# The last stores of an attention and channel-mix kernel: one queue for all turned results, and the very last result transposed by TensorE in two halves

## The chip, the cores and the metric

The kernel runs on one core of a Trainium2 chip. The metric is the device time of one execution in microseconds (us), the median of several runs; lower is better. Engines are named as in the profile: PE is TensorE (PEld its weight loads), DVE is VectorE, ACT is ScalarE, POOL is GpSimd, SP is SyncE. SPq and ACTq are the instruction queues of SP and ACT, from which they issue transfers (DMAs).

## The reference

For eight batches, an attention with a packed middle step is followed by a channel mix. Inputs are float32: q, k, v of (8, 8, 576, 64), p of (8, 8, 32, 64), w_k (512, 1024), w_v (1024, 512), w_r (512, 512).

```python
p_packed = sm_attn(p, k, v)            # 32 packed rows for each head
out = sm_attn(q, p_packed, p_packed)   # (8, 8, 576, 64)
x = out.transpose(0, 2, 1, 3).reshape(8, 576, 512)
x_prev = x shifted by one token, zero in front
xk = mu_k * x + (1 - mu_k) * x_prev
xr = mu_r * x + (1 - mu_r) * x_prev
k = maximum(xk @ w_k, 0)
r = 1 / (1 + exp(-(xr @ w_r)))
result = r * ((k * k) @ w_v)           # (8, 576, 512) float32
```

## The kernel before

The 4608 tokens are taken in nine groups of 512 (TB). Seven groups go one after the other; the last two, called the pair (`first` and `second`), are multiplied together in a scheme of seven products of half-size blocks (A11, S2, S3, S1, A12, S4, A22). The products with w_k are made in `keys_of_pair`, the products with w_v in `values_of_pair`, which is the end of the kernel. Each float32 product is made of three matmuls of a high and a low part (lines 1802 to 1804).

The order of the work is written by a planner, the class `Flow`. Every part of the work is a Python generator that yields an engine and an estimated duration; the planner always takes the part that can begin first (ties by rank, then by age) and so fixes the order of the instructions on each engine. The instructions themselves then wait for one another by semaphores that the framework places. SP's transfers are issued by `load` (line 221), each costing the planner's "queue" an estimated time; `back_to_issue()` lets a part issue its next transfer as soon as the queue is free and not only when the last one has landed.

In `values_of_pair` the products hold 128 output columns in the partitions and 512 tokens in the free dimension, so that a result has to be turned before it is stored. One turned result is 128 columns by 512 tokens. There are eight of them, in this order, each with j = 0 and then j = 1: S1 (tokens of `second`, upper columns), A12 (`first`, lower columns), S4 (`first`, upper columns), A22 (`second`, lower columns). The tile that is stored is named sigs in the profile for S1, sig for A12 and S4, and turned for A22. `made_of` ends each of them: DVE adds the part kept from earlier products (line 1747, not for A22), multiplies by the sigmoid (line 1750, or line 1741 for A22), turns blocks of 32 by 32 (line 1752), and then four transfers of 64 KB store the four groups of 32 columns (lines 1755 to 1764). A transfer writes runs of 32 floats (128 bytes).

For S1, A12 and S4 all four transfers are issued by SP. For A22 (`n is None`) the transfers with a = 0 and 2 are issued by SP and those with a = 1 and 3 by ACT:

```python
if n is None and a % 2:
    yield "scalar", 0.1, None, None
    nc.scalar.dma_start(to, what)
```

`ms[0..3]` are four PSUM banks: Z uses the first two, Y the last two. A22 accumulates in Z; Y was last used by A12.

Of the kernel before, what the change touches and what calls it, by code (L numbers as in the profile page):

```python
# [8 lines left out]
F32 = mybir.dt.float32  # L9
# [3 lines left out]
ALU = mybir.AluOpType  # L13
# [160 lines left out]
def attn_pack_channel_mix(ctx: ExitStack, tc: tile.TileContext, q, k, v, p, mu_k, mu_r, w_k, w_v, w_r, out):  # L174
    nc = tc.nc
# [3 lines left out]
    P = 128  # L179
# [7 lines left out]
    TB = 512  # L187
    NB = B * S // TB
    NT = TB // P
# [5 lines left out]
    flow = Flow()  # L195
# [4 lines left out]
    def vec(n, after=None):  # L200
        return "vector", 0.07 + 1.04e-3 * n, after, None
# [4 lines left out]
    def act(n, after=None, table=None):  # L206
        return "scalar", 0.14 + 0.72e-3 * n, after, table
# [4 lines left out]
    def pe(us, after=None):  # L212
        return "tensor", us, after, None

    def load(dst, src, issue, us, beside=False):
        if beside:
            yield "gpsimd", 0.6, None, None
            nc.gpsimd.dma_start(dst, src)
            return
        yield "queue", issue, None, None  # L220
        nc.sync.dma_start(dst, src)
        begin = max(flow.free.get("dma", 0.0), flow.t + 0.46)
        flow.free["dma"] = begin + us
        flow.free["queue"] = max(flow.free["queue"], begin - 2.0)
        flow.now.t = begin + us + LANDS
# [16 lines left out]
    ps = ctx.enter_context(tc.tile_pool(name="ps", bufs=1, space=bass.MemoryType.PSUM))  # L242
# [7 lines left out]
    def tile_(shape, dtype, tag, slot, name=None):  # L250
        return sb.tile(shape, dtype, name=name or tag, tag=f"{tag}{slot}")

    def banks(slot):
        return ps.tile([P, 2, 512], F32, name="pa", tag=f"pa{slot}")
# [19 lines left out]
    ident = const.tile([P, P], F32, name="ident")  # L274
# [166 lines left out]
    def back_to_issue():  # L441
        flow.now.t = flow.free["queue"]
# [701 lines left out]
    sqs, sigs = {}, {}  # L1144
# [126 lines left out]
    def channel_mix():  # L1271
        for i in range(NB - 2):
            if i == 0:
                flow.spawn(first_mix(), RANK_MIX)
            yield from gates(i)
            yield from keys(i)
            mixes(i + 1)
            yield from values(i)
        flow.set("values")
        for i in PAIR:  # L1280
            yield from gates_across(i)
        flow.set("gates")
        yield from keys_of_pair()
        yield from values_of_pair()
# [61 lines left out]
    T2, T3, T4, T1 = "T2", "T3", "T4", "T1"  # L1346

    def small_tile(slot, dtype, name):
        tag, j = slot
        o = LEAD[tag][j]  # L1350
        return tile_([P, S], dtype, tag, j, name)[:, o:o + WP]
# [364 lines left out]
    def values_of_pair():  # L1716

        first, second = PAIR
        ms = []
        for _ in range(4):  # L1720
            ms.append((yield from flow.take("m")))
        Z, Y = ([ps.tile([P, TB], F32, name="pv", tag=f"m{slot}") for slot in ms[n:n + 2]] for n in (0, 2))
        X = [None, None]
        parts_of = {}

        def kept(n, j):
            slot = yield from flow.take("keep")
            x = small_tile(slot, F32, "kept")
            parts_of[n, j] = slot, x
            yield act(TB)  # L1730
            nc.scalar.copy(x, Z[j])
            flow.set(("kept v", n, j))

        def made_of(bank, j, i, h, n):
            yield from flow.wait(("sig", i, 2 * h + j))
            sig = sigs[i, 2 * h + j]
            if n is None:
                slot = yield from flow.take("keep")
                x = small_tile(slot, F32, "turned")
                yield vec(TB)  # L1740
                nc.vector.tensor_tensor(sig, bank[j], sig, op=ALU.mult)
                sig, x = x, sig
            else:
                yield from flow.wait(("kept v", n, j))
                slot, x = parts_of[n, j]
                yield vec(TB)
                nc.vector.tensor_tensor(x, bank[j], x, op=ALU.add)
                flow.set(("read v", n, j))
                yield vec(TB)
                nc.vector.tensor_tensor(x, x, sig, op=ALU.mult)  # L1750
            yield vec(TB)
            nc.vector.transpose(sig.rearrange("p (a b) -> p a b", b=32), x.rearrange("p (a b) -> p a b", b=32))
            if n is not None:
                flow.give("keep", slot)
            for a in range(4):
                d = DH * h + P * j + 32 * a
                to = out[i * TB:(i + 1) * TB, d:d + 32].rearrange("(b k) i -> k b i", k=32)
                what = sig[32 * a:32 * a + 32].rearrange("k (b i) -> k b i", i=32)
                if n is None and a % 2:
                    yield "scalar", 0.1, None, None  # L1760
                    nc.scalar.dma_start(to, what)
                else:
                    yield from load(to, what, 0.5, 0.3)
                    back_to_issue()

        def of_wv(f0, o):
            return lambda u, j: tuple(wvs[f0 + u][:, x, o + j * P:o + (j + 1) * P] for x in range(2))

        def of_wr(home):
            flat = home.rearrange("p c d -> p (c d)").rearrange("p (h u d) -> p h u d", h=2, u=HF)  # L1770
            return lambda u, j: tuple(flat[:, x, u, j * P:(j + 1) * P] for x in range(2))

        def of_wk(u, j):
            o = DH * (u % 2) + j * P
            return tuple(x[:, u // 2, o:o + P] for x in (wk_h, wk_l))

        passes = (
            ("A11", None, of_wv(0, 0), Z, True, None, lambda j: kept("P1", j)),
            ("S2", T2, of_wr(wr_h), Z, False, ("kept v", "P1"), lambda j: kept("U2", j)),
            ("S3", T3, of_wr(wr_l), Z, False, ("kept v", "U2"), lambda j: kept("U3", j)),  # L1780
            ("S1", T1, of_wv(0, DH), X, True, None, lambda j: made_of(X, j, second, 1, "U3")),
            ("A12", None, of_wv(HF, 0), Y, True, None, lambda j: made_of(Y, j, first, 0, "P1")),
            ("S4", None, of_wv(HF, DH), X, False, ("read v", "U3"), lambda j: made_of(X, j, first, 1, "U2")),
            ("A22", T4, of_wk, Z, False, ("kept v", "U3"), lambda j: made_of(Z, j, second, 0, None)),
        )
        for name, weights_, ws, bank, opens, before, evict in passes:
            if weights_:
                yield from flow.wait(("tv", weights_))
            if bank[0] is None:
                for j in range(2):  # L1790
                    X[j] = banks((yield from flow.take("pa")))[:, 0, :]
            for j in range(2):
                if before:
                    yield from flow.wait((*before, j))
                for u in range(HF):
                    yield from flow.wait(("vf", name, u))
                    slot, xh, xl = forms_v[name, u]
                    yield pe(0.685)
                    flow.now.t -= flow.LAG
                    wh, wl = ws(u, j)  # L1800
                    go = not opens
                    nc.tensor.matmul(bank[j], wh, xh, start=(opens and u == 0), stop=False, skip_group_check=go)  # L1802
                    nc.tensor.matmul(bank[j], wh, xl, start=False, stop=False, skip_group_check=go)  # L1803
                    nc.tensor.matmul(bank[j], wl, xh, start=False, stop=(u == HF - 1), skip_group_check=go)  # L1804
                    if j:
                        flow.give("ring", slot)
                flow.spawn(evict(j), 0, flow.t + flow.LAG)
# [98 lines left out]
```

## Time and profile before

| what | us |
|---|---|
| median of 3 runs | 588.04 (587.76 to 588.65) |
| the profiled execution, its own time | 586.39 |
| its span (first to last instruction) | 584.6 |
| PE busy | 567.9 |
| DVE busy | 435.7 |
| ACT busy | 349.0 |

The span is what the trace shows; the execution's own time is 1.79 us longer than its span, and it lies 1.65 us under the median of the runs. PE is busy for 97% of the span, and the mean granted clock is 0.994. In the fortieth and last slice of the span (14.6 us) PE's busy share is only 0.2, and the DMA engines' is 0.4.

### The profile page before, as it was taken

Reading aid. Unit: us, or ns where it says so; the run is one execution under the profiler, and the core shown is the slowest. Engines: PE = TensorE matmul, PEld = TensorE weight load, DVE = VectorE, ACT = ScalarE, POOL = GpSimd, SP = SyncE. Lnnn points to the kernel's source line nnn. Section 1 sums busy time; section 2 is a strip of 40 time slices with the busy share of each in tenths; the row PEclk is TensorE's granted clock in tenths of the full one; section 3 lists DMA queues with packets and bytes.
Section 4 is the critical chain, followed back from the end, with each engine's and each line's share of the span. In section 5 each row is a group of like instructions: output and inputs, shape, how many; then the busy total and the mean of one; then the engine's idle time right before and its main releaser. Section 6 shows DMA issues by size and latency. Waiting matters only on the chain.

```text
span 584.6 us, 10714 instructions
## 1 busy us (share of the span) xinstructions
PE 567.9 (97%) x4067; PEld 447.1 (76%) x4067; DVE 435.7 (75%) x804; ACT 349.0 (60%) x625; POOL 13.2 (2%) x41
## 2 busy tenths in 40 slices
PE   8999999899999999999999999999999999999992
PEld 7877777687788778877877777777788888888881
DVE  1999789956892889088829788559896985858991
ACT  5678983765744584268427752746568755578710
POOL 3000000000000000000000000000000100100000
PEclk9999999999999999999999999999999999999997
DMA  8987440863366364407640763730122340600034
GB/s 304 339 244 230 112 66 11 191 143 59 76 134 169 49 142 91 146 5 153 117 127 16 155 141 102 158 98 1 64 82 73 110 161 19 217 0 1 1 64 81
DMA packets 182612, 65.08 MB, mean 111 GB/s; under 512 B 154008, under 2 KB 172576, under 8 KB 182304
## 3 DMA queue, kind: packets, MB, share of 16 engines
q1 hardware_dynamic: 178208, 59.80, 41.0%
q0 software_dynamic: 2240, 4.33, 2.5%
q8 instruction: 32, 0.52, 0.4%
q10 hardware_dynamic: 2112, 0.26, 0.3%
q14 instruction: 20, 0.16, 0.1%
HBM read 47.19 MB, written 17.17 MB: 110 GB/s over the span
## 4 chain that ended last, share of the span: by engine, by line
PE 78%; DVE 12%; ACT 4%; issue 2%; DMA 1%; SPq 0%; POOL 0%; DVEq 0%; POOLq 0%; ACTq 0%
PE ph L1162 8%; PE ph L1163 7%; PE ph L1164 7%; PE pvo L1244 7%; PE pvo L1245 7%; PE pvo L1246 7%; PE pr L1214 4%; PE pr L1216 4%; PE pr L1215 3%; PE pa L706 2%; DVE x L1117 2%; PE pv L1804 2%; PE pv L1802 2%; PE pv L1803 2%; PE pa L898 1%
## 5 line engine op out<-in xcount | busy, mean ns | idle before, releaser
L1162 PE MATMUL ph<-xk,wk_h 128*128 128x512 f32 x224 | 90.8, 405 | 0.0
L1244 PE MATMUL pvo<-wv,sq 128*128 128x512 f32 x224 | 89.0, 397 | 0.0
L1163 PE MATMUL ph<-xk,wk_h 128*128 128x512 f32 x224 | 87.6, 391 | 0.0
L1164 PE MATMUL ph<-xk,wk_l 128*128 128x512 f32 x224 | 87.4, 390 | 0.0
L1245 PE MATMUL pvo<-wv,sq 128*128 128x512 f32 x224 | 87.4, 390 | 0.0
L1246 PE MATMUL pvo<-wv,sq 128*128 128x512 f32 x224 | 87.3, 390 | 0.0
L1174 ACT ACTIVATE r<-ph 128x512 f32<-128x512 f32 x56 | 33.6, 600 | 46.5 <-PE ph L1164 44.5
L1162 PEld LDWEIGHTS ph<-xk,wk_h 128*128 128x128 f32 x224 | 42.1, 188 | 14.2 <-issue 5.9
L1244 PEld LDWEIGHTS pvo<-wv,sq 128*128 128x128 f32 x224 | 42.1, 188 | 13.6 <-issue 4.9
L1117 DVE SCALAR_TENSOR_TENSOR x<-xt,mus,x 128x128 f32<-128x128 f32 (+6 forms) x100 | 46.5, 505 | 4.0 <-ACT x L1111 3.8
L1164 PEld LDWEIGHTS ph<-xk,wk_l 128*128 128x128 f32 x224 | 42.1, 188 | 9.0
L1246 PEld LDWEIGHTS pvo<-wv,sq 128*128 128x128 f32 x224 | 42.1, 188 | 8.9
L1245 PEld LDWEIGHTS pvo<-wv,sq 128*128 128x128 f32 x224 | 42.1, 188 | 8.1
L1111 ACT ACTIVATE x<-xt,mus 128x128 f32<-128x128 f32 (+6 forms) x100 | 47.6, 523 | 1.2 <-DVE sq L1190 1.2
L1163 PEld LDWEIGHTS ph<-xk,wk_h 128*128 128x128 f32 x224 | 42.2, 188 | 7.6 <-DVE xk L1056 0.2
L1214 PE MATMUL pr<-wr_h,xr 128*128 128x512 f32 x112 | 45.4, 405 | 0.7 <-ACT xr L1137 0.7
L1216 PE MATMUL pr<-wr_h,xr 128*128 128x512 f32 x112 | 43.9, 392 | 0.8 <-DVE xr L1139 0.8
L1190 DVE TENSOR_TENSOR sq<-r,sq 128x512 fp32r<-128x512 f32 x56 | 38.0, 678 | 8.8 <-ACT sq L1185 4.8
L1215 PE MATMUL pr<-wr_l,xr 128*128 128x512 f32 x112 | 43.8, 391 | 0.0
L1072 ACT COPY xt<-pa 128x576 f32<-128x576 f32 x28 | 30.6, 1174 | 10.8 <-PE pa L898 10.7
L1177 ACT ACTIVATE r<-r 128x512 f32<-128x512 f32 x56 | 35.5, 634 | 1.2
L1188 DVE CAST sq<-r 128x512 fp32r<-128x512 f32 x40 | 16.7, 417 | 22.5 <-ACT r L1177 21.9
(266 smaller groups left out, 1071.8 us busy)
## 6 DMA issues: line engine op xcount, KB each, us to landing
vt<-in_v SPq DMA_DIRECT2D x14, 512.0 KB, 4.5
raw<-in_k SPq DMA_DIRECT2D x96, 72.0 KB, 2.7
raw<-in_q SPq DMA_DIRECT2D x96, 72.0 KB, 2.7
out<-sig SPq DMA_DIRECT2D x23, 256.0 KB, 2.7
st<-in_moe_w_k SPq DMA_DIRECT2D x8, 512.0 KB, 9.5
st<-in_moe_w_v SPq DMA_DIRECT2D x8, 512.0 KB, 5.6
far<-at SPq DMA_DIRECT2D x12, 288.0 KB, 2.6
aTd<-far SPq DMA_DIRECT2D x12, 256.0 KB, 2.9
```

Source lines behind the costliest of these rows:

```text
L1111: nc.scalar.mul(x32[:, o:o + n], xts[b, c][:, 1 + s:1 + s + n], mus[:, j, c:c + 1])
L1117: nc.vector.scalar_tensor_tensor(x32[:, o:o + n], xts[b, c][:, s:s + n], mus[:, j + 1, c:c + 1], x32[:, o:o + n], op0=ALU.mult, op1=ALU.add,)
L1162: nc.tensor.matmul(ph, wk_h[:, c, fs], xh, start=(c == 0), stop=False)
L1163: nc.tensor.matmul(ph, wk_h[:, c, fs], xl, start=False, stop=False)
L1164: nc.tensor.matmul(ph, wk_l[:, c, fs], xh, start=False, stop=(c == NC - 1))
L1190: nc.vector.tensor_tensor(hl[:, 1, :], r, hl[:, 0, :].bitcast(F32), op=ALU.subtract)
L1214: nc.tensor.matmul(pr, xh[:, ts_], wr_h[:, c, :], start=(c == 0), stop=False)
L1215: nc.tensor.matmul(pr, xh[:, ts_], wr_l[:, c, :], start=False, stop=False)
L1216: nc.tensor.matmul(pr, xl[:, ts_], wr_h[:, c, :], start=False, stop=(c == NC - 1))
L1244: nc.tensor.matmul(pv[t], sh, wvs[f][:, 0, :], start=(f == 0), stop=False)
L1245: nc.tensor.matmul(pv[t], sh, wvs[f][:, 1, :], start=False, stop=False)
L1246: nc.tensor.matmul(pv[t], sl, wvs[f][:, 0, :], start=False, stop=(f == NF - 1))
```

## The change

Two things are changed, both in `values_of_pair`. First, all four transfers of each turned result are issued by SP through `load`; ACT issues none. Second, the very last result (A22 with j = 1) is no longer made by `made_of` but by `very_last`. It is multiplied by the sigmoid in two halves of 256 tokens; each half is transposed by PE in two blocks of 128 by 128 into a PSUM bank that Y used, copied to SBUF by ACT (first half) or DVE (second half), and stored by one transfer of 128 KB with runs of 128 floats (512 bytes). Its DVE turn and its four transfers of 64 KB are gone.

```diff
-                if n is None and a % 2:
-                    yield "scalar", 0.1, None, None
-                    nc.scalar.dma_start(to, what)
-                else:
-                    yield from load(to, what, 0.5, 0.3)
-                    back_to_issue()
+                yield from load(to, what, 0.5, 0.3)
+                back_to_issue()
+
+        def very_last(j):
+            yield from flow.wait(("sig", second, j))
+            sig = sigs[second, j]
+            slot = yield from flow.take("tmp")
+            o = tile_([P, NT, P], F32, "tmp", slot, "natural")
+            two = NT // 2
+            for g in range(2):
+                own = slice(g * two * P, (g + 1) * two * P)
+                yield vec(TB // 2, after=0.0)
+                nc.vector.tensor_tensor(sig[:, own], Z[j][:, own], sig[:, own], op=ALU.mult)
+                flow.spawn(natural(j, g, sig, o), 0)
+
+        def natural(j, g, sig, o):
+            two = NT // 2
+            tp = ps.tile([P, two, P], F32, name="tn", tag=f"m{ms[2 + g]}")
+            yield pe(0.24)
+            for x in range(two):
+                t = g * two + x
+                nc.tensor.transpose(tp[:, x, :], sig[:, t * P:(t + 1) * P], ident)
+            what = o[:, g * two:(g + 1) * two, :]
+            yield (vec if g else act)(two * P)
+            (nc.vector.tensor_copy if g else nc.scalar.copy)(what, tp)
+            t0 = second * TB + g * two * P
+            yield from load(
+                out[t0:t0 + two * P, P * j:P * (j + 1)].rearrange("(x p) d -> p x d", p=P), what, 0.5, 0.3,
+            )
...
-            ("A22", T4, of_wk, Z, False, ("kept v", "U3"), lambda j: made_of(Z, j, second, 0, None)),
+            ("A22", T4, of_wk, Z, False, ("kept v", "U3"), lambda j: very_last(j) if j else made_of(Z, j, second, 0, None)),
```

## Rows read from the trace of the kernel before

**Rows 1.** The chain that ended last, in order of time: start, duration, what.

```profile
572.98 0.24 PE pv L1804
573.24 0.70 DVE sigs L1741
573.97 0.71 DVE turned L1752
```

**Rows 2.** Timeline of SP's queue, one transfer a row: start, duration, engine, line, what.

```profile
563.16 0.32 SPq L221 DMA_DIRECT2D out<-sig  x1
...
565.20 0.43 SPq L221 DMA_DIRECT2D out<-sig  x1
565.68 0.49 SPq L221 DMA_DIRECT2D out<-sig  x1
573.80 0.32 SPq L221 DMA_DIRECT2D out<-sig  x1
...
575.25 0.51 SPq L221 DMA_DIRECT2D out<-sig  x1
576.66 0.32 SPq L221 DMA_DIRECT2D out<-sig  x1
...
579.79 0.43 SPq L221 DMA_DIRECT2D out<-turned  x1
...
581.53 0.48 SPq L221 DMA_DIRECT2D out<-turned  x1
```

**Rows 3.** What SP's queue waited for from 540 us on: total, times, longest.

```profile
SPq L221 <- DMA out<-turned: 8.5, 2, 7.6
```

**Rows 4.** Timeline of ACT's queue at the end.

```profile
571.99 0.93 ACTq L1761 DMA_DIRECT2D out<-turned  x2
574.71 0.38 ACTq L1761 DMA_DIRECT2D out<-turned  x1
```

**Rows 5.** Transfers: count, KB, median us to landing; last row: all stores after 540.

```profile
out<-sig SPq DMA_DIRECT2D x23, 256.0 KB, 2.7
...
farT<-hw SPq DMA_DIRECT2D x8, 256.0 KB, 2.1
...
out<-turned ACTq DMA_DIRECT2D x4, 64.0 KB, 1.9
...
out<-turned SPq DMA_DIRECT2D x1, 64.0 KB, 2.1
...
DMA to landing us min/median/max: 1.7/1.9/3.9
```

**Rows 6.** Timeline of DVE: the turns of S4's two results and A22's first.

```profile
566.54 0.71 DVE L1752 STREAM_TRANSPOSE sig<-kept 128x512 f32<-128x512 f32 x1
...
569.26 0.71 DVE L1752 STREAM_TRANSPOSE sig<-kept 128x512 f32<-128x512 f32 x1
...
571.25 0.71 DVE L1752 STREAM_TRANSPOSE turned<-sigs 128x512 f32<-128x512 f32 x1
```

**Rows 7.** Timeline near 18 and 5 us: a half-size multiply, pairs of transposes.

```profile
17.64 0.42 DVE L602 TENSOR_TENSOR pm<-pa,rs 128x256 f32<-128x256 f32 x1 [0.52 <-PE pa L584]
...
18.12 0.44 PE L613 MATMUL pa<-ident,pm 128*128 128x128 f32 x2
...
4.76 0.64 PE L503 MATMUL pa<-ident,rows 128*128 128x128 f32 x2
```

**Rows 8.** Groups by line and form: count, busy us, mean ns, idle before.

```profile
L508 ACT COPY pt<-pa 128x256 f32<-128x256 f32 x1 | 0.4, 372 | 2.3 <-PE pa L503 2.3
...
L729 DVE TENSOR_TENSOR pm<-pa,rs 128x128 f32<-128x128 f32 x7 | 2.0, 291 | 23.6 <-PE pa L706 23.6
...
L1731 ACT COPY kept<-pv 128x512 f32<-128x512 f32 x6 | 3.5, 581 | 0.1
```

**Rows 9.** Stretch by windows: length, busy of each engine, clock, DMA share, GB/s.

```profile
573.60:575.80 2.20, 0.00 (x0) 0.00 (x0) 1.05 (x2) 0.00 (x0) 0.00 (x0) 1.00 0.53 92
577.50:580.80 3.30, 0.00 (x0) 0.00 (x0) 0.00 (x0) 0.00 (x0) 0.00 (x0) 0.50 0.70 120
```

## The prediction, made before the change was run

> **What bounds the kernel now.** I read the page first: PE is busy almost throughout, but in the last slice hardly, so the place of this change, the tail, has a limit of its own. The chain of waits [rows 1] then shows where PE stops: its last matmul ends at 573.22, DVE multiplies until 573.94 and turns until 574.68. After that no engine computes, yet the span lasts until 584.6: some 10 us of tail hold only transfers. The timeline of SP's queue [rows 2] shows why. SP issues the four transfers of a result about 0.51 us apart (563.16 to the next result's 565.20, 2.04 for four). After the second transfer of A12's second result, which ends at 566.17, it issues nothing until 573.80: 7.63 us. It pauses again from 575.76 to 576.66, 0.90 us. The view of SP's waits puts both, 8.5 us in two waits, on the landing of out<-turned [rows 3], although SP's own turned transfers come only at 579.79 and later. So these are ACT's. ACT's first two are issued from 571.99 on, the next at 574.71 [rows 4]; with 1.9 us to landing [rows 5] the first lands at about 573.9 and the third at 576.6, which is where SP goes on, within 0.1.
>
> So SP's older stores wait for ACT's newer ones. The data cannot ask for that, since they are different results. I take it for a wait that the framework places: transfers of SP and ACT share a few completion semaphores in turn, and one that gets a semaphore used by another must wait until that other has landed. The trace shows the wait and its end, the sharing is my inference. Behind the waiting transfer stand, on the same queue, the rest of A12, all of S4 and SP's share of A22: results that DVE had finished at 567.25, 569.97 and 571.96 [rows 6] are issued only after 574. The end is set by SP's queue: last issue 581.53, landing 2.1 later at 583.63 [rows 2, 5], then 0.97 of closing steps to 584.6.
>
> **Part 1: four transfers leave ACT's queue.** This removes whatever SP waits for on that side: both pauses, 8.5 us of SP's time. What it adds is issue time on SP. A22's first result has four transfers there where it had two, 1.0 us more, while the very last result has two where it had two. The cover for the added time is SP's idle time between results. Worked forward at 0.51 a transfer: A12's second result is issued from 565.20 to 567.24; S4's first, ready at 567.25, from 567.3 to 569.3; S4's second, ready at 569.97, from 570.0 to 572.05; A22's first, ready at 571.96, from 572.1 to 574.1. SP keeps up with DVE, and it is free before the very last result needs it. If that cover were gone, each transfer issued late would cost its 0.51. Semaphores still go round, but if the same one comes back after eight transfers, that is 4.1 us later at this pace, longer than any landing here (1.9, at most 3.9 [rows 5]), so I cost waits among SP's own transfers at nothing. The DMA engines are not the limit either: with SP alone issuing at full pace they were busy for 0.70 of the time at 120 GB/s [rows 9].
>
> A rule speaks against this part. The Trainium skill ("DMA: Bandwidth & Descriptors", section "Issuing engines are not separate DMA queues") says that all transfers run on the same 16 DMA engines whichever engine issues them, and that using several issuers saves only the sequencer's issue time. By that rule ACT's help could only have saved time, and taking it away could only cost; the trace disagrees, since it shows ACT's transfers holding SP for 8.5 us. By the rule the sum would be that of the rival on the slower side, below; by the rows it is a gain.
>
> **Part 2: the very last result by halves.** All of it lies on the path that sets the end, since nothing is left to cover it. Removed: the multiply of 0.70, the turn of 0.71 [rows 1], and four transfers. Added, from PE's end at 573.22:
>
> - The half multiply: 0.42 from a multiply of the same size out of PSUM [rows 7]; bounds 0.35 (half of the 0.70) and 0.70 (no saving). I take 0.42: first half 573.24 to 573.66, second 573.69 to 574.11.
> - Two transposes: PE began 0.06 after DVE ended and took 0.44 for a pair [rows 7]. A pair at about 5 us took 0.64 [rows 7], which is the bound. The granted clock is still 1.00 (2.4 GHz) from 573.6 to 575.8, with PE already idle [rows 9], so I take 0.44. First half 573.72 to 574.16, second 574.17 to 574.61.
> - The copies out of PSUM: ACT 0.37 for this size, bounds 0.29 and 0.58 from a smaller and a larger operation [rows 8]. No DVE copy of float32 out of PSUM is shown; its bounds are 0.29 (a multiply of half the size [rows 8]) and 0.42 (a multiply of this size [rows 7]). I take 0.40, near the upper, as the size is the same. ACT 574.20 to 574.57, DVE 574.65 to 575.05.
> - SP: the first half is issued at 574.62 and takes up to 0.49; the second at 575.15.
> - Landing of 128 KB: not shown in this stage. 64 KB took 1.9 to 2.1, 256 KB 2.1 or 2.7 [rows 5]. I take 2.2, because the first half's data is still under way; bounds 1.9 and 2.7.
>
> New waits are those of PE for DVE, of ACT and DVE for PE, and of SP for the copies. Behind each stands only the other half, as these are the last instructions of their engines. The PSUM banks that are reused were last read for A12, whose second result was on its way out at 565.20 [rows 2], so they cost nothing.
>
> **The sum.** The last issue moves from 581.53 to 575.15, 6.38 earlier; the landing is 0.1 longer: 6.3 us. The span becomes 584.6 - 6.3 = 578.3, the profiled execution 586.39 - 6.3 = 580.1. The runs' median lies 1.65 above that execution; taking the gain off the median gives 588.04 - 6.3 = 581.7, or 1.1% less.
>
> All lower bounds together put the second half's issue at 574.9 and its landing at 576.8: a gain of 6.8, 581.2. All upper bounds put it at 576.05 and 578.75: a gain of 4.9, 583.1.
>
> **The rivals.**
>
> Slower: the pause is not ACT's doing. SP would stop after the fourteenth transfer of this stage for a reason of its own, such as a limit on what its queue holds, and the agreement with ACT's landings would be chance. Then SP still goes on at 573.80 and pauses a second time; the queue behind has 16 transfers where it had 14, 1.0 us more, and the last is larger (0.1 to 0.6): 589.2 to 589.7, about 589.4. That is also what is left of the change if ACT's queue only ever saved issue time. For it: the semaphores themselves are not named in the view of waits, and a releaser is inferred. Against it: two pauses end within 0.1 us of two different landings, the seven transfers from 576.66 to 579.79 begin 0.52 apart without a pause, and earlier transfers had landed 1.9 us after issue, so nothing was full. It decides if SP's third transfer of A12's second result still starts later than 573. Chance 0.06.
>
> Faster by less, through the landing: the last transfer takes as long as the slowest store of this stage, 3.9 [rows 5], because five results now follow one another without a pause and the large halves queue behind them. Then it lands at 579.05, the span ends at 580.0, a gain of 4.6: 583.4. Against it: 0.70 busy at full pace, with landings near 1.9. Chance 0.06.
>
> The pause is only shortened: some of SP's transfers get a semaphore whose last user is still to come in another queue. POOL's transfers of the pair were issued long before, and no other queue stores here, so I know of no such one; times from 583.5 to 587. Chance 0.03.
>
> **How the numbers follow.** The forecast, the pauses gone and PE's path as the tail, has 0.85: 581.7. The range holds it with its bounds, 581.0 to 583.2, the lower end with 0.2 for the scatter of the runs (which reach 0.3 below their median). What a measurement of this kernel can tell from no change is about 0.2%, 1.2 us. Faster by more than that: 0.85 + 0.06 + 0.03, less a little for what I do not see, 0.92. Slower: most of the 0.06, as its price of 1.4 is just over that bound, 0.05. Within: 0.03.
>
> **What would show it.** In the timeline of SP's queue no gap over 1 us between 565 and 574 except before S4's second result, and SP's waits name no transfer but only DVE and ACT; A22's first result issued by 574.2; two 128 KB transfers at about 574.6 and 575.15; PE with four transposes from 573.7 to 574.6; ACT's queue with no transfer; a span of 578.3. Wrong would be a gap of several us on SP in the same place (the slower rival), transposes that begin after 574.2 (a whole multiply before them), or a last landing more than 2.7 after its issue.

## The result and the profile after

The changed kernel takes 580.05 us (median of 5 runs, 579.65 to 581.26) against 587.76 of the kernel before (5 runs). The ratio over all these runs is 0.9877, 95% interval 0.9858 to 0.9895; it goes with the means, which differ by 7.2, and not with the two medians, which differ by 7.7. In a second comparison the medians were 580.19 against 587.27, ratio 0.9885 (0.987 to 0.990); there the means differ by 6.8. The forecast was faster, 581.7, with a range of 581.0 to 583.2: the direction is right, the time lies below the range.

In the profiled execution the span is 577.9 where it was 584.6. The first view to compare is the timeline of SP's queue in the changed kernel, against [rows 2].

```profile
562.90 0.32 SPq L221 DMA_DIRECT2D out<-sig  x1
...
564.95 0.44 SPq L221 DMA_DIRECT2D out<-sig  x1
565.43 0.49 SPq L221 DMA_DIRECT2D out<-sig  x1
565.96 0.51 SPq L221 DMA_DIRECT2D out<-sig  x1
...
569.74 0.32 SPq L221 DMA_DIRECT2D out<-sig  x1
...
571.79 0.43 SPq L221 DMA_DIRECT2D out<-turned  x1
572.26 0.49 SPq L221 DMA_DIRECT2D out<-turned  x1
573.11 0.32 SPq L221 DMA_DIRECT2D out<-turned  x1
...
574.34 0.42 SPq L221 DMA_DIRECT2D out<-natural  x1
574.86 0.41 SPq L221 DMA_DIRECT2D out<-natural  x1
```

The third transfer of A12's second result follows the second at once (565.96), where it came 7.63 us after the second had ended. S4's second result goes out at 569.74 and A22's first at 571.79, each within 0.1 of the end of its turn, and the last transfer is issued at 574.86 where the last one was issued at 581.53. What SP waited for from 540 us on, against [rows 3]: total, times, longest.

```profile
SPq L221 <- DVE sigs L1752: 78.3, 2, 76.7
SPq L221 <- DVE sig L1752: 0.9, 2, 0.5
SPq L1925 <- DMA out<-natural: 0.8, 2, 0.5
```

Line 1925 is the end of the program; no transfer of line 221 waits for a transfer any more. The chain that ended last, against [rows 1], shows the new path of the very last result:

```profile
572.73 0.24 PE pv L1827
...
572.99 0.44 DVE sigs L1771
...
573.47 0.78 PE tn L1780 x4
...
574.28 0.42 DVE natural L1783
```

PE ends its matmuls at 572.97; the last transfer is issued 1.89 later and lands 1.9 after that.

**A measure without the scatter ahead of the tail.** The change touches only the tail, but executions also differ ahead of it. The same DVE instruction of the first token group, near 56 us, in the kernel before, in the changed kernel, and in one of the experiments below (the very last result whole):

```profile
56.55 0.68 DVE L1190 TENSOR_TENSOR sq<-r,sq 128x512 fp32r<-128x512 f32 x1
```

```profile
56.37 0.68 DVE L1190 TENSOR_TENSOR sq<-r,sq 128x512 fp32r<-128x512 f32 x1
```

```profile
57.55 0.69 DVE L1190 TENSOR_TENSOR sq<-r,sq 128x512 fp32r<-128x512 f32 x1
```

The three kernels do the same work up to there, and the starts differ by 1.2 us. So every tail below is also given from the first transfer of A12's first result (563.16 before [rows 2], 562.90 after) to the end of the span: 584.6 - 563.16 = 21.4 before, 577.9 - 562.90 = 15.0 after, which is 6.4 less. The kernel before was traced once, so whatever is particular to that one tail is in every gain below.

### The profile page after: what moved, and what is told of

Read it like the earlier page. It is cut to its first block, busy times and chain, and to the rows that moved or that the text cites. A ratio compares the mean times of both kernels' runs of the same rounds, so it can differ in the third digit from the quotient of the medians.

```text
span 577.9 us, 10721 instructions
## 1 busy us (share of the span) xinstructions
PE 568.4 (98%) x4071; PEld 447.2 (77%) x4071; DVE 435.5 (75%) x805; ACT 349.4 (60%) x626; POOL 13.3 (2%) x41
## 4 chain that ended last, share of the span: by engine, by line
PE 78%; DVE 14%; ACT 4%; issue 2%; DMA 1%; SPq 1%; DVEq 0%; ACTq 0%
PE ph L1162 8%; PE ph L1163 8%; PE ph L1164 8%; PE pvo L1244 7%; PE pvo L1245 7%; PE pvo L1246 7%; PE pr L1214 4%; PE pr L1216 4%; PE pr L1215 4%; DVE m L303 2%; PE pa L706 2%; DVE x L1117 2%; PE pv L1827 2%; PE pv L1826 2%; PE pv L1825 2%
## 5 line engine op out<-in xcount | busy, mean ns | idle before, releaser
L1188 DVE CAST sq<-r 128x512 fp32r<-128x512 f32 x40 | 16.7, 417 | 21.9 <-ACT r L1177 21.3
```

## The experiments

Seven kernels were run. The table puts them together; "tail" is the measure just given, and "gain in the tail" is against 21.4.

| kernel | first transfer of A12 | span | tail | gain in the tail | ratio of times to before, 95% interval |
|---|---|---|---|---|---|
| before | 563.16 | 584.6 | 21.4 | | |
| changed | 562.90 | 577.9 | 15.0 | 6.4 | 0.9877, 0.9858 to 0.9895 |
| 1: the queue alone | 563.42 | 579.3 | 15.9 | 5.6 | 0.9891, 0.9878 to 0.9905 |
| 2: the last result alone | 563.93 | 584.1 | 20.2 | 1.3 | 0.9977, 0.9966 to 0.9987 |
| 3: POOL for ACT | 563.19 | 579.6 | 16.4 | 5.0 | one run: 581.36 us |
| 4: one transfer by ACT | 563.98 | 585.3 | 21.3 | 0.1 | 0.9987, 0.9978 to 0.9996 |
| 5: changed, again | 563.23 | 578.2 | 15.0 | 6.5 | 0.9885, 0.987 to 0.990 |
| 6: the last result whole | 565.24 | 580.8 | 15.6 | 5.9 | 0.9893, 0.9876 to 0.9909 |
| 7: one early transfer by ACT | 563.55 | 578.5 | 15.0 | 6.5 | 0.9889, 0.9874 to 0.9904 |

### 1: the queue alone

The kernel before with the first part of the change only.

```diff
-                if n is None and a % 2:
-                    yield "scalar", 0.1, None, None
-                    nc.scalar.dma_start(to, what)
-                else:
-                    yield from load(to, what, 0.5, 0.3)
-                    back_to_issue()
+                yield from load(to, what, 0.5, 0.3)
+                back_to_issue()
```

> Part 1 alone: all transfers of turned results by SP, the very last result still turned by DVE and stored by four transfers of 64 KB. Theory A (SP was held by waits for ACT's transfers, through completion semaphores that the two queues share): no pause in SP's queue after 566; the very last result is ready at 574.7, its four issues start from 574.75 to 576.2, the last lands 2.1 later, span 579.4, that is 5.2 below the 584.6 of before and 1.5 above the 577.9 of the changed kernel. Theory B (SP stops for a reason of its own, and the gain comes from the shorter path of the very last result): the pause until about 573.8 stays and the span is about 586.

Measured: span 579.3, with no pause for a transfer. The end of its SP queue:

```profile
566.49 0.51 SPq L221 DMA_DIRECT2D out<-sig  x1
...
574.97 0.32 SPq L221 DMA_DIRECT2D out<-turned  x1
...
576.42 0.49 SPq L221 DMA_DIRECT2D out<-turned  x1
```

The third transfer of A12's second result is on time (566.49), and the very last result's four are issued as soon as DVE has turned it. This one part carries 5.6 of the 6.4: theory A holds. Over it, the second part is worth 15.9 - 15.0 = 0.9, not the 1.5 that was expected: the last issue comes 1.89 after PE's end instead of 2.94 (PE ended at 573.48 here), 1.05 earlier, but the end follows its last issue by 3.04 instead of 2.88.

### 2: the last result alone

The changed kernel with ACT's share of A22's first result put back.

```diff
-                yield from load(to, what, 0.5, 0.3)
-                back_to_issue()
+                if n is None and a % 2:
+                    yield "scalar", 0.1, None, None
+                    nc.scalar.dma_start(to, what)
+                else:
+                    yield from load(to, what, 0.5, 0.3)
+                    back_to_issue()
```

> Part 2 alone: the very last result by halves through PE, but A22's first result still has two of its four transfers issued by ACT. Theory A: ACT's two transfers still take semaphores that older transfers of SP need next. One pause is left, until ACT's first transfer has landed at about 573.8; it comes before S4's first result (567.3) and not within A12's second, since two transfers fewer stand in the rotation. Then ten transfers at 0.52 and the two halves follow: last issue 579.5, span 582.4, a gain of 2.2. Theory B (the last result's path is the gain): a gain of over 5, span under 579.5.

Measured: span 584.1. SP's queue, and the wait in it:

```profile
567.53 0.49 SPq L221 DMA_DIRECT2D out<-sig  x1
574.62 0.32 SPq L221 DMA_DIRECT2D out<-sig  x1
...
580.74 0.41 SPq L221 DMA_DIRECT2D out<-natural  x1
```

```profile
SPq L221 <- DMA out<-turned: 6.5, 1, 6.5
```

One pause, before S4's first result, as theory A places it; ACT's first transfer was issued at 572.77 and SP goes on 1.85 later. The span missed the forecast by 1.7: 0.77 is ahead of the tail (563.93 against 563.16), 0.42 is a gap in SP's queue behind the pause (see the last section), and from the last issue to the end it took 3.4 instead of 2.9 (the two halves took 2.3 to landing, by the median). The 1.3 that this part gains alone are not those of a shorter path, which does not set the end here: the second pause of 0.90 is gone with two of ACT's transfers, and 12 transfers stand behind the pause where there were 14, so that SP needs 6.12 from the end of the pause to its last issue (574.62 to 580.74) instead of 7.73.

### 3: POOL for ACT

The kernel before with ACT's four transfers issued by POOL.

```diff
-                    yield "scalar", 0.1, None, None
-                    nc.scalar.dma_start(to, what)
+                    yield "gpsimd", 0.6, None, None
+                    nc.gpsimd.dma_start(to, what)
```

> The kernel before with the four transfers of ACT issued by POOL's queue, whose completion semaphores are others. Theory A: what holds SP is the shared semaphores and not that a second queue has transfers in flight, so the pauses after 566 are gone: SP's last issue at about 575.2, POOL's last at about 575.5 with 3.1 (up to 5) to landing, span 579.6 to 581.5. Theory B or any cause that lies in the use of a second queue: SP still pauses until 573.8 or later and the span is 584 or more.

Measured, in one run: span 579.6, as theory A had it. SP's queue after A12's second result, and POOL's last transfer:

```profile
566.26 0.51 SPq L221 DMA_DIRECT2D out<-sig  x1
...
575.11 0.48 SPq L221 DMA_DIRECT2D out<-turned  x1
```

```profile
575.66 0.65 POOL L1761 DMA_DIRECT2D out<-turned  x1
```

A second queue with transfers under way at the same time does not hold SP. What holds it lies between SP and ACT. The transfers of POOL signal none of the semaphores that those of SP signal.

### 4: one transfer by ACT

The changed kernel with the first half of the very last result issued by ACT.

```diff
-            yield from load(
-                out[t0:t0 + two * P, P * j:P * (j + 1)].rearrange("(x p) d -> p x d", p=P), what, 0.5, 0.3,
-            )
+            to = out[t0:t0 + two * P, P * j:P * (j + 1)].rearrange("(x p) d -> p x d", p=P)
+            if not g:
+                yield "scalar", 0.1, None, None
+                nc.scalar.dma_start(to, what)
+            else:
+                yield from load(to, what, 0.5, 0.3)
```

> The changed kernel with one transfer moved: the first half of the very last result is issued by ACT, which has just copied it. By the issue time alone this is nothing or a gain of up to 0.4 (span 577.5 to 577.9), since the two halves no longer follow one another on SP. Theory A: the one transfer of ACT stands in the rotation before S4's first result, whose fourth transfer must wait until it has landed: SP pauses from about 568.9 to 576.3, then ten transfers follow at 0.52, last issue about 581, span 583.5 to 584.3: one transfer takes back nearly all of the gain.

Measured: span 585.3; in the tail, 6.3 of the 6.4 are gone, and by the medians of the runs 0.6 is left (587.2 to 586.58). SP's queue around its pause, the wait, and ACT's one transfer:

```profile
569.19 0.51 SPq L221 DMA_DIRECT2D out<-sig  x1
577.28 0.32 SPq L221 DMA_DIRECT2D out<-sig  x1
...
582.14 0.53 SPq L221 DMA_DIRECT2D out<-natural  x1
```

```profile
SPq L221 <- DMA out<-natural: 7.6, 1, 7.6
```

```profile
575.43 0.42 ACTq L1788 DMA_DIRECT2D out<-natural  x1
```

The fourth transfer of S4's first result, whose data DVE had turned more than 8 us earlier, waits for the landing of a transfer of the last result, issued at 575.43 and landed 1.8 later. Nine more transfers stand behind it on SP. The place is the forecast one; the span is 1.0 over the forecast's upper end, of which 0.8 is ahead of the tail (563.98).

The compiled program says why this transfer, and the trace's records of the transfers carry the same semaphores. Each transfer on SP and ACT signals one of eight completion semaphores, which are given in turn over both queues together, and a transfer waits until the one before it on the same semaphore has landed. The order in which they were given, from A12's second result on (ACT's transfer is placed there although it is issued after S4's turns):

```
ACT  last result, half 0      semaphore 2
SP   A12 second, a = 0 to 3   semaphores 3, 4, 5, 6
SP   S4 first,   a = 0 to 3   semaphores 7, 0, 1, 2   <- a = 3 waits for ACT's landing
```

### 5: the changed kernel again

> The changed kernel once more, with many runs of the kernel before beside it, to size the gain against the scatter of the runs. Theory A (the gain is the sum of the tail: 6.3 predicted, 6.7 between the two profiled executions, of which 0.25 lies ahead of the tail): the medians differ by 6.2 to 6.8, a ratio of 0.9885 to 0.9895; the 7.7 of the first comparison then is scatter of the base. Theory B (something ahead of the tail has become faster too): 7.2 or more again, 0.988 or less.

Measured: 580.19 against 587.27, ratio 0.9885 (0.987 to 0.990); span 578.2, tail 15.0. The medians are 7.1 apart, near theory B's bound (the means 6.8), but the interval takes in the tail's 6.5 (1 - 6.5/587.27 = 0.9889) as well as 7.2; the tail of the profile repeats to 0.1. Ahead of the tail this execution is not faster (563.23 against 563.16).

### 6: the very last result whole

The changed kernel without the halves.

```diff
-            two = NT // 2
-            for g in range(2):
-                own = slice(g * two * P, (g + 1) * two * P)
-                yield vec(TB // 2, after=0.0)
-                nc.vector.tensor_tensor(sig[:, own], Z[j][:, own], sig[:, own], op=ALU.mult)
-                flow.spawn(natural(j, g, sig, o), 0)
+            yield vec(TB, after=0.0)
+            nc.vector.tensor_tensor(sig, Z[j], sig, op=ALU.mult)
+            flow.spawn(natural(j, 0, sig, o), 0)
 
         def natural(j, g, sig, o):
-            two = NT // 2
+            two = NT
```

> The changed kernel with the very last result in one piece: one multiply of 512 tokens, four transposes into one bank, one copy by ACT, one transfer of 256 KB. Theory A: the path from PE's end is 0.70 + 0.06 + 0.7 + 0.04 + 0.58 + 0.05, so the transfer is issued 2.15 after PE's end where the second half was issued 1.89 after it, and lands 0.2 to 0.5 later after its issue: span 0.5 to 0.8 longer than the changed kernel's with an equal end of PE, 578.4 to 578.7. Rival (the halves only add steps): no longer, or shorter, as one transfer and three steps fewer are issued.

Measured: span 580.8 in an execution that was 2.1 late ahead of the tail (565.24). Its chain, from PE's end on:

```profile
575.06 0.24 PE pv L1824
575.30 0.02 issue
575.33 0.70 DVE sigs L1768
576.03 0.04 issue
576.07 0.67 PE tn L1777 x4
576.74 0.02 issue
576.77 0.59 ACT natural L1780
```

From PE's end (575.30) to the end of the span it takes 5.5, where the changed kernel takes 577.9 - 572.97 = 4.9: the halves are worth 0.6, within the forecast 0.5 to 0.8. In experiments 5 and 7, which have the halves too, it takes 4.9 as well. The medians (580.95 against 580.19) point the same way, but the intervals overlap, so the traces alone show it.

### 7: one early transfer by ACT

The changed kernel with another transfer moved to ACT.

```diff
+                if (i, h, j, a) == (second, 1, 0, 3):
+                    yield "scalar", 0.1, None, None
+                    nc.scalar.dma_start(to, what)
+                    continue
                 yield from load(to, what, 0.5, 0.3)
                 back_to_issue()
```

> The changed kernel with one transfer moved to ACT as in the earlier run, but an early one: the fourth of S1's first result, which ACT can issue at about 557.4. Theory A: the transfer of SP that gets its semaphore next is one of A12's first result at 563.2, and ACT's has landed by 559.4: no pause, span as the changed kernel's, 577.6 to 578.4. Rival (any transfer on ACT's queue in this stage costs, whenever it is issued): a pause or a span over 580.

Measured: span 578.5, tail 15.0, no wait for a transfer. ACT's transfer, and the one of SP that takes its semaphore next:

```profile
557.43 0.41 ACTq L1761 DMA_DIRECT2D out<-sigs  x1
```

```profile
563.91 0.49 SPq L221 DMA_DIRECT2D out<-sig  x1
```

A transfer on ACT's queue costs nothing in itself. It costs when the program places it in the rotation ahead of transfers that are issued long before it. No experiment pointed to a version that beats the changed kernel by more than the measurement can tell.

## Why the prediction was right, and where it was wrong

**The pauses: right.** Both were ACT's doing and both went. That semaphores are shared was called an inference; experiments 3, 4 and 7 show it from three sides: a second queue with other semaphores does no harm, one late transfer of ACT does all of it, and an early one does none. The rotation was assumed to come back after eight, which it does. The trace of the kernel before has it too, once the semaphores of its transfers are read: SP's transfers at 573.80 and 576.66 wait for those that ACT's first and third transfer signal, and these landed at 573.79 and 576.65.

**SP's issue time: right.** SP kept up with DVE without ACT's help, as worked forward at 0.51 a transfer; A22's first result went out from 571.79 to 573.96.

**The path of the very last result: right.** From PE's end to the second half's issue 1.93 was forecast and 1.89 measured: the multiplies took 0.76 for both halves (0.87 forecast, 573.24 to 574.11), the four transposes 0.78 (0.89, 573.72 to 574.61), DVE's copy 0.42 (0.40).

**The landing: mis-sized.** 2.2 was taken "because the first half's data is still under way"; it took 1.9. The closing steps behind it took 1.1 instead of 0.97, so that from the last issue to the end 3.17 was forecast and 3.04 measured; this term did not decide the miss.

**The sum: right; the base: wrong.** The tail's gain was forecast at 6.3 and measured at 6.4 and 6.5. The step that failed is the last of the sum: "The runs' median lies 1.65 above that execution; taking the gain off the median gives 588.04 - 6.3 = 581.7". The 588.04 was the median of three runs that scattered by 0.9. With more runs the same kernel took 587.76 (5 runs, those three among them), 587.2 (18) and 587.27 (7), so the base was up to 0.8 too high. The lower end of the range, 581.0, allowed 0.2 for scatter and could not hold that.

Taken at 0.8, the base is about half of the miss of 1.65 (581.7 - 580.05). With 587.27 in its place the forecast is 581.0 and the lower end of the range 580.2, and the measured 580.05 and 580.19 would still lie at or just below that end. Some 0.2 more is the tail, which gained 6.5 and not 6.3; the rest is that the runs differ by more than the tails do: 7.1 to 7.7 by the medians, 6.8 to 7.2 by the means, against 6.4 to 6.5. That rest is inside the intervals (the forecast ratio, 581.7/588.04 = 0.9892, lies in both); whether any of it is real was not settled.

The other figure of the prediction, 586.39 - 6.3 = 580.1 for the profiled execution, is what the medians of the changed kernel came to (580.05, 580.19), but by luck: 586.39 lies below every one of those 30 runs of the kernel before (the fastest took 586.54), and the changed kernel's own profiled execution took 579.65. One sum of bounds is also off: added up step by step, the upper bounds put the second half's issue at about 575.9 and not at 576.05, which changes nothing here.

**The rivals.** "The pause is not ACT's doing" is refuted by experiments 1 and 4. The long landing of 3.9 did not come: in the changed kernel the medians of the landings are 1.9 to 2.2. Nor was the pause only shortened; it was gone. The rule of the Trainium skill ("DMA: Bandwidth & Descriptors", "Issuing engines are not separate DMA queues") that a second issuer saves only issue time did not decide here. Experiment 7 agrees with it (ACT's early transfer neither cost nor gained); experiment 4 does not, since one transfer cost 6.3 us.

## What to carry to other kernels

When a queue pauses on the landing of a transfer that it has no data from, look at the completion semaphores: if two queues share them in rotation, a late transfer on one queue can hold everything behind an early one on the other, and moving it to the busier queue can be faster than letting an idle engine help. Shortening the last result's path pays only once the queue no longer sets the end; here it was worth 0.9 us of the 6.4. Take a forecast's base from as many runs as there are, and give the range the scatter of that base as well as the bounds of the sum.

## What the runs showed of the hardware that was not expected

The two halves moved faster than the transfers of short runs. The rate in the changed kernel from 574.8 to 578, in 40 slices of 0.08 us, where the halves move:

```profile
GB/s 157 58 14 13 11 6 154 346 326 365 307 128 39 250 333 339 365 250 71 0 0 0 0 0 0 0 0 0 0 0 0 0 0 0 0 0 0 0 0 0
```

And in the kernel before from 580.5 to 582, in 40 slices of 0.0375 us, where two transfers of A22's first result move:

```profile
GB/s 181 171 89 52 21 0 7 82 123 167 208 188 191 188 174 181 123 72 31 10 4 58 99 171 191 198 208 171 195 185 134 89 41 10 0 0 0 0 0 218
```

Runs of 512 bytes went at up to 365 GB/s, 128 KB in some 0.5 us; runs of 128 bytes went at up to 208 GB/s, 64 KB in some 0.5 us too. (The 120 GB/s of [rows 9] is a mean that has the gaps between transfers in it.) The two halves did not run into one another, with a slice of 39 GB/s between them. So it fits that twice the bytes landed no later, 1.9 after the issue, than 64 KB did.

SP pauses for about 0.4 after the 26th of its transfers in this stage (counted from S1's first), whichever that is, and no wait is shown for it (0.34 to 0.42 in the eight traces where it can be seen; in experiment 3 SP waits for DVE there). In the changed kernel it is between A22's second and third transfer (572.75 to 573.11, above). In experiment 7, where SP has one transfer fewer, it moved by one:

```profile
573.44 0.50 SPq L221 DMA_DIRECT2D out<-turned  x1
574.28 0.32 SPq L221 DMA_DIRECT2D out<-turned  x1
```

It follows the count of SP's transfers and not the data. In each of the eight traces 8 KB move on a queue that the profile calls "instruction" 0.7 to 0.9 us after SP has gone on; whether that belongs to the pause, and what causes it, was not tried.
